# Attention and a feed-forward block on one core: the first feed-forward product of the later passes computed with seven half-deep products for eight, its weight blocks read from DRAM

## The chip, the cores and the metric

The kernel runs on one core of one Trainium2 chip. The metric is the device time of one execution in microseconds (us), as the median of the runs shown. Engines are called as the profile calls them: PE is the matrix engine (PEld its weight loads), DVE the vector engine, ACT the scalar engine, POOL the general-purpose engine, SP the engine that issues nearly all of this kernel's DMAs.

## The reference, cut to what matters

```python
mask   = q_bucket[:, :, :, None] == k_bucket[:, :, None, :]
scores = np.where(mask, scale * np.matmul(q, k.transpose(0, 1, 3, 2)), -1000000000.0)
...
x = attn_out.transpose(0, 2, 1, 3).reshape(B * S, H * D)     # 3072 x 512
h = x @ w_in                                                 # 512 x 2048
g = np.where(pos, h, np.where(neg, 0.0, (h + beta) ** 2 / (4.0 * beta)))
return (g @ w_out).astype(np.float32)                        # 2048 x 512
```

There are 4 batches of 768 tokens and 8 heads of 64. The change touches only how `h = x @ w_in` is computed for batches 1, 2 and 3.

## The kernel before, in words

All matrix products are float32 by splitting: each operand is held as a high part and a low part in the fast 32-bit matmul format (F32R), and a product is the sum of three matmuls, high by high, high by low and low by high.

First comes the attention of all 32 heads, `NU` = 12 work units to a head; it is not changed. Beside it the weights are converted from 64-bit to 32-bit floats: `WeightSplit.steps` makes for each of 16 blocks of `w_in` and of `w_out` a list of steps (DMA of the raw words, four DVE steps and one ACT step, the cast to the high part on ACT, the subtraction that gives the low part), and `conv` hangs each step on a work unit of the attention by a table of offsets. Some blocks are put to DRAM (`stage`, tensors `wd`) and fetched later. The blocks of `w_in` end in `wih` and `wil` (12 tiles of their own, four in tiles that attention gives up), those of `w_out` in `woh` and `wol`.

Then `ffn` runs over units (c, f): c is one of 8 chunks of `CH` = 384 tokens (two chunks to a batch), f one of 16 blocks of 128 hidden columns. `gemm1` issues 12 matmuls of 384 columns (four quarters of the contraction by three) into one of two PSUM banks `h`. ACT makes `t` and `z` from the bank (two ACTIVATEs), DVE finishes the function (one SCALAR_TENSOR_TENSOR, one TENSOR_TENSOR), ACT casts `ghi`, DVE subtracts to `glo`. `gemm2` issues 9 matmuls of 512 columns into three of six PSUM banks `y`; it is called `GLAG` = 3 units behind `gemm1`, so a unit's function has three units of time. `ffn_order` runs the two chunks of batch 0 interleaved (32 units, in which the last `w_out` blocks are still converted), then chunks 2 to 7 one after the other (96 units).

The normalised input of a chunk is made during the chunk before it: `load_x` issues DMAs of the raw rows and of two broadcast factors (`xe`, `xr`), `XMaker.make` has four parts per quarter (DVE, POOL, ACT cast, POOL subtraction). The order on every engine is the order in which the program writes it; each engine takes its instructions strictly in that order, and `prep` and `post` are lists of small pieces that are written just before or just after a unit's `gemm1`.

Of the kernel before, what the change touches and what calls it, by code (L numbers as in the profile page):

```python
# [13 lines left out]
I32 = mybir.dt.int32  # L14
# [27 lines left out]
class WeightSplit:  # L42
# [10 lines left out]
    def steps(self, src, shape, hi, lo, cp, stage=None, low=None):  # L53
# [39 lines left out]

        if stage is None:
            return [s0, s1, s2, s3, s4, s5, s6]

        def put():
            nc.sync.dma_start(out=stage, in_=st["sq"])
# [396 lines left out]
NCT = DM // P  # L495
NF = H * S // P
# [71 lines left out]
def ffn(ctx, tc, wih, wil, woh, wol, xm, xa, xb, out, prep, post):  # L568
# [3 lines left out]
    ps_h = ctx.enter_context(tc.tile_pool(name="ps_h", bufs=2, space=PSUM, reuse_waits="tile"))  # L572
    ps_y = ctx.enter_context(tc.tile_pool(name="ps_y", bufs=6, space=PSUM, reuse_waits="tile"))
    mh = xp.tile([P, 1], F32, name="mh")
# [3 lines left out]
    xc = (xp.tile([P, NCT, CH], F32R, name="xhi"), xp.tile([P, NCT, CH], F32R, name="xlo"))  # L578
    xs = [xa, xb] + [xc, xa] * ((NCH - 2) // 2)

    def piece(name):
        return xp.tile([P, CH], F32, name=name, bufs=2)

    def load_x(c, ct):
        if ct == 0:
            xm.load_sv(c, xp.tile([P, NCT, 2], F32, name="xsv"))
        if c == 1:
            xm.load_raw(c, ct, piece(("xraw", "xraw", "xe", "xr")[ct]))
        else:
            xm.load_raw(c, ct, piece("xraw"))  # L590
            xm.load_er(c, ct, piece("xe"), piece("xr"))

    def gemm1(c, f):
        hi, lo = xs[c]
        ps = ps_h.tile([P, 512], F32, name="h")
        n = 0
        for ct in range(NCT):
            cs = slice(ct * P, (ct + 1) * P)
            for w, x in ((wih[f], hi), (wih[f], lo), (wil[f], hi)):
                nc.tensor.matmul(out=ps[:, 0:CH], lhsT=w[:, cs], rhs=x[:, ct, :], start=(n == 0),  # L600
                                 stop=(n == 3 * NCT - 1))
                n += 1
        t = gp.tile([P, CH], F32, name="t")
        z = gp.tile([P, CH], F32, name="z", bufs=3)
        nc.scalar.activation(out=t, in_=ps[:, 0:CH], func=AF.Relu, scale=0.5, bias=mh)  # L605
        nc.scalar.activation(out=z, in_=t, func=AF.Relu, scale=1.0, bias=m1)  # L606
        nc.vector.scalar_tensor_tensor(out=t, in0=t, scalar=1.0, in1=t, op0=ALU.min, op1=ALU.mult)  # L607
        nc.vector.tensor_tensor(out=z, in0=t, in1=z, op=ALU.add)
        g = [None, None, z]
        to_hi.append(g)  # L610
        return g

    to_hi, to_lo = [], []

    def g_hi(left):

        while len(to_hi) > left:
            g = to_hi.pop(0)
            g[0] = gp.tile([P, CH], F32R, name="ghi", bufs=GLAG)
            nc.scalar.copy(out=g[0], in_=g[2])  # L620
            to_lo.append(g)

    def g_lo():
        while to_lo:
            g = to_lo.pop(0)
            g[1] = gp.tile([P, CH], F32R, name="glo", bufs=GLAG)
            nc.vector.tensor_tensor(out=g[1], in0=g[2], in1=g[0].bitcast(F32), op=ALU.subtract)  # L627

    ys = {}

    def gemm2(c, f, g):
        ghi, glo, _ = g
        if f == 0:
            ys[c] = [ps_y.tile([P, 512], F32, name="y") for _ in range(CH // P)]
        for m in range(CH // P):
            ms = slice(m * P, (m + 1) * P)
            for k, (g_, w) in enumerate(((ghi, woh[f]), (ghi, wol[f]), (glo, woh[f]))):
                nc.tensor.matmul(out=ys[c][m], lhsT=g_[:, ms], rhs=w, start=(f == 0 and k == 0),  # L638
                                 stop=(f == NFT - 1 and k == 2))
            if f == NFT - 1:  # L640
                r0 = c * CH + m * P
                if c == NCH - 1 and m == CH // P - 1:
                    for n, cp in ((0, nc.vector.tensor_copy), (1, nc.scalar.copy)):
                        cs = slice(n * DM // 2, (n + 1) * DM // 2)
                        ot = piece(("xraw", "xe")[n])[:, 0:DM // 2]
                        cp(out=ot, in_=ys[c][m][:, cs])
                        nc.sync.dma_start(out=out[r0:r0 + P, cs], in_=ot)
                    continue
                ot = xp.tile([P, DM], F32, name="ot", bufs=2)
                nc.scalar.copy(out=ot, in_=ys[c][m])  # L650
                nc.sync.dma_start(out=out[r0:r0 + P, :], in_=ot)
# [7 lines left out]
    for ct in reversed(range(NCT)):  # L659
        prep[0].insert(0, (load_x, (1, ct)))  # L660
# [204 lines left out]
```

## Time and profile before

| | us |
|---|---|
| median of 3 runs (lowest to highest) | 1019.07 (1018.93 to 1019.59) |
| profiled execution, its own time | 1019.4 |
| its span | 1017.3 |
| attention ends, first unit of the feed-forward block starts | 473.9 |
| first unit of chunk 2 starts | 603.5 |
| PE busy | 993.6 of 1017.3 |
| DVE, ACT, POOL busy | 695.4, 647.4, 396.5 |

In the rows of the trace the first number is a start in us from the span's start, then a duration. Durations of matmuls overlap, since they are pipelined; the pace of a run of matmuls is read from the chain of work, which gives a start, the length of a piece and its count. The granted clock of PE was 1.00 in every stretch looked at.

### The profile page before, as it was taken

To read this page: it belongs to the slowest core of one execution; us is meant where nothing else is said; L and a number is where in the kernel's file an instruction comes from. 1 tells how busy PE (TensorE), PEld (TensorE's weight loads), DVE (VectorE), ACT (ScalarE), POOL (GpSimd) and SP (SyncE) were. 2 spreads that over 40 slices of the span, in tenths; PEclk is the share of its full clock that TensorE was granted. 3 is DMA by queue.
4 is the path that set the end of the run, shared out by engine and by line. 5 is a ranking of instruction groups with operands and counts; after the bars stand their busy time and mean duration, and the time that the engine had idled before them with its cause. 6 is when DMAs were issued, how large, how long until landed. Compare 5 with 4: busy or idle time off the path is not lost.

```text
span 1017.3 us, 15246 instructions
## 1 busy us (share of the span) xinstructions
PE 993.6 (98%) x5180; PEld 918.3 (90%) x5180; DVE 695.4 (68%) x1106; ACT 647.4 (64%) x1430; POOL 396.5 (39%) x460
## 2 busy tenths in 40 slices
PE   5899999999999999999999999999999999999998
PEld 4789999999999999989999999999999999999997
DVE  7678999999999998895877644544535445355332
ACT  5779988998899998887555544444444444444433
POOL 6666777777887777565000210201202102011000
PEclk9999999999999999999999999999999999999999
DMA  3645666766666666535113102102021021020000
GB/s 93 166 108 155 165 167 175 182 172 168 156 168 164 152 162 171 134 102 166 63 62 109 62 19 79 47 21 81 24 78 47 1 79 47 22 80 24 32 1 32
DMA packets 52806, 100.11 MB, mean 98 GB/s; under 512 B 12920, under 2 KB 34040, under 8 KB 52728
## 3 DMA queue, kind: packets, MB, share of 16 engines
q1 hardware_dynamic: 52512, 99.14, 35.9%
q8 instruction: 41, 0.67, 0.3%
q14 instruction: 37, 0.30, 0.1%
q10 hardware_dynamic: 216, 0.00, 0.0%
HBM read 57.90 MB, written 16.04 MB: 73 GB/s over the span
## 4 chain that ended last, share of the span: by engine, by line
PE 89%; DVE 4%; ACT 3%; DMA 2%; issue 1%; POOL 0%; SPq 0%; DVEq 0%; ACTq 0%
PE y L638 26%; PE h L600 26%; PE smax L258 7%; PE s L298 6%; PE o L332 6%; PE o L330 6%; PE o L331 5%; PE s L297 5%; DVE nm L262 2%; PE o L178 2%; DMA t<-te 1%; DVE nm L359 1%; DMA wraw<-in_w_in_dram 1%; DVE pl L39 0%; ACT ph L306 0%
## 5 line engine op out<-in xcount | busy, mean ns | idle before, releaser
L605 ACT ACTIVATE t<-h,mh 128x384 f32<-128x384 f32 x128 | 74.5, 582 | 272.8 <-PE h L600 272.2
L607 DVE SCALAR_TENSOR_TENSOR t<-t 128x384 f32<-128x384 f32 x128 | 72.6, 567 | 253.5 <-ACT z L606 253.5
L306 ACT ACTIVATE ph<-s 128x384 fp32r<-128x384 f32 x380 | 188.2, 495 | 47.0 <-PE s L298 40.5
L262 DVE TENSOR_REDUCE nm<-smax 128x1 f32<-128x768 f32 x186 | 176.4, 948 | 18.4 <-PE smax L258 16.3
L39 POOL TENSOR_TENSOR pl<-pf,ph 128x384 fp32r<-128x384 f32 x128 | 142.0, 1115 | 77.4 <-ACT pf L311 75.3
L39 DVE TENSOR_TENSOR pl<-s,ph 128x384 fp32r<-128x384 f32 x256 | 135.7, 545 | 13.7 <-ACT s L311 10.0
L297 PE MATMUL s<-t 128*128 128x384 f32 x384 | 132.1, 344 | 0.8 <-DVE t L212 0.8
L550 POOL TENSOR_TENSOR xraw<-xraw,xr 128x384 f32<-128x384 f32 x24 | 24.7, 1027 | 274.8 <-DVE xraw L547 274.8
L298 PE MATMUL s<-t 128*128 128x384 f32 x384 | 130.2, 339 | 0.8 <-DMA t<-te 0.8
L332 PE MATMUL o<-pl,va 128*128 128x386 f32 x384 | 130.4, 340 | 0.2 <-DVE pl L39 0.2
L330 PE MATMUL o<-ph,va 128*128 128x386 f32 x384 | 130.1, 339 | 0.0
L331 PE MATMUL o<-ph,vb 128*128 128x386 f32 x384 | 129.5, 337 | 0.0
L311 ACT ACTIVATE s<-s 128x384 f32<-128x384 f32 x252 | 125.0, 496 | 0.0
L600 PE MATMUL h<-t,wih 128*128 128x384 f32 x480 | 122.9, 337 | 1.0 <-ACT t L605 1.0
L638 PE MATMUL y<-t,ghi 128*128 128x512 f32 x384 | 120.2, 394 | 0.0
L258 PE MATMUL smax<-t 128*128 128x384 f32 x372 | 101.4, 353 | 5.4 <-DVE nm L262 4.5
L600 PEld LDWEIGHTS h<-t,wih 128*128 128x128 f32 x480 | 88.0, 188 | 6.2 <-ACT t L605 1.4
L627 DVE TENSOR_TENSOR glo<-z,ghi 128x384 fp32r<-128x384 f32 x128 | 89.5, 699 | 0.2 <-ACT ghi L620 0.2
L258 PEld LDWEIGHTS smax<-t 128*128 128x128 f32 x372 | 64.0, 188 | 21.9 <-DVE nm L262 20.8
L638 PEld LDWEIGHTS y<-t,ghi 128*128 128x128 f32 x384 | 71.4, 188 | 11.4
L606 ACT ACTIVATE z<-t,m 128x384 f32<-128x384 f32 x128 | 79.0, 617 | 4.1
L600 PE MATMUL h<-t,wil 128*128 128x384 f32 x240 | 80.9, 337 | 0.0
(130 smaller groups left out, 2106.6 us busy)
## 6 DMA issues: line engine op xcount, KB each, us to landing
t<-t SPq DMA_DIRECT2D x60, 384.0 KB
raw<-in_qk_dram SPq DMA_DIRECT2D x15, 768.0 KB
wraw<-in_w_in_dram SPq DMA_DIRECT2D x16, 512.0 KB
wraw<-in_w_out_dram SPq DMA_DIRECT2D x16, 512.0 KB
xd<-xs SPq DMA_DIRECT2D x32, 192.5 KB
vraw<-in_v_dram SPq DMA_DIRECT2D x16, 384.0 KB
out_dram<-ot SPq DMA_DIRECT2D x23, 256.0 KB
xraw<-xd SPq DMA_DIRECT2D x26, 192.0 KB
```

The lines of the kernel that those rows point to most:

```text
L39: eng.tensor_tensor(out=out, in0=a, in1=b, op=ALU.subtract)
L258: nc.tensor.matmul(out=smax[hd][:, hf, 0:HS], lhsT=t2[:, 0, h, i * P:(i + 1) * P], rhs=t2[:, 1, h, hf * HS:(hf + 1) * HS], start=True, sto ...
L262: nc.vector.tensor_reduce(out=nmp(hd)[:, i:i + 1], in_=smax[hd][:, :, 0:HS], axis=AX.XY, op=ALU.max, negate=True)
L297: nc.tensor.matmul(out=ps[:, 0:HS], lhsT=t1[:, 1, h, ks], rhs=t1[:, 0, h, sl], start=True, stop=False)
L298: nc.tensor.matmul(out=ps[:, 0:HS], lhsT=t2[:, 1, h, ks], rhs=t2[:, 0, h, sl], start=False, stop=True)
L306: nc.scalar.activation(out=ph[:, 0:HS], in_=ps[:, 0:HS], func=AF.Exp, scale=SCALE)
L311: nc.scalar.activation(out=pf, in_=ps[:, 0:HS], func=AF.Exp, scale=SCALE)
L330: nc.tensor.matmul(out=o, lhsT=wa, rhs=ph, start=(jj == 0), stop=False)
L331: nc.tensor.matmul(out=o, lhsT=wb, rhs=ph, start=False, stop=False)
L332: nc.tensor.matmul(out=o, lhsT=wa, rhs=pl, start=False, stop=(jj == NJ - 1))
L600: nc.tensor.matmul(out=ps[:, 0:CH], lhsT=w[:, cs], rhs=x[:, ct, :], start=(n == 0), stop=(n == 3 * NCT - 1))
L638: nc.tensor.matmul(out=ys[c][m], lhsT=g_[:, ms], rhs=w, start=(f == 0 and k == 0), stop=(f == NFT - 1 and k == 2))
```

## The change

For batches 1 to 3 the first product is taken over pairs: two blocks of hidden columns (2i and 2i+1), two halves of the contraction and the two chunks of a batch make a 2 by 2 by 2 scheme of eight half-deep products; the kernel now forms seven (`PRODUCTS`), each of 6 matmuls of 384 columns. This needs sums of inputs (four per half of the contraction, `x_sum`), sums of weights (four blocks out of four, `w_sum`) and sums of results: three products accumulate in PSUM on top of an earlier one, ACT copies one bank out and DVE adds five times per seven products.

Weights: the converted 32-bit blocks are also written to DRAM (`wq`, for the 12 blocks that were not staged before, at offset 16 of the table). In the first 32 units the kernel writes the three plain half blocks of each pair to DRAM tensors `wc` (`w_plan`, `w_plain`), fetches pairs back into a scratch tile `tmp` (`w_get`), forms the four sums (`w_sum`), splits them (`w_hi` on ACT, `w_lo` on DVE) and writes them to `wc` (`w_put`): pairs 0 to 2 in the first 32 units (the put of pair 2 stands at product 0), pairs 3 to 7 during products 0 to 28. Each product then reads its weight block (128 by 512 floats, high and low) from `wc` into a ring of 9 slots, 9 products ahead (`w_load`).

Inputs: 14 operands (7 combinations, high and low) per half of the contraction are made one batch ahead, on DVE and ACT alone (`x_plan`: raw rows, factors `x_er`, `x_norm`, `x_sum`, `x_hi`, `x_lo`); POOL has no work left in this part.

Second product: its matmuls go into one queue (`queue_out`), and `issue` writes 4 to 6 of them behind each product, 36 per seven products. There are 3 x 8 x 7 = 168 products.

PE, one unit of the last chunk before. `h` is the PSUM bank of the first product, `y` those of the second, `x12` is a count:

```order
L638 MATMUL y<-wol_6035,ghi 128x512
L638 MATMUL y<-woh_6034,glo 128x512
L600 MATMUL h<-t_1_78,t_2_76 128x384 x12
L638 MATMUL y<-woh_6036,ghi 128x512
L638 MATMUL y<-wol_6037,ghi 128x512
L638 MATMUL y<-woh_6036,glo 128x512
```

PE in the change, two products in the first of the three later batches; `wbig` holds operands, `t_1_75` is a slot of the ring:

```order
L867 MATMUL h_6066<-wbig,t_1_75 128x384 x6
L657 MATMUL y<-woh_6045,ghi 128x512
L657 MATMUL y<-wol_6046,ghi 128x512
L657 MATMUL y<-woh_6045,glo 128x512
L657 MATMUL y<-woh_6047,ghi 128x512
L657 MATMUL y<-wol_6048,ghi 128x512
L867 MATMUL h_6065<-wbig,t_1_75 128x384 x6
L657 MATMUL y<-woh_6047,glo 128x512
```

A group of 12 has become groups of 6 that alternate between the two banks, with five matmuls of the second product between them.

DVE, two units before (`t`, `z`, `glo` are the function's tiles, `xraw` a piece of input being normalised):

```order
L607 SCALAR_TENSOR_TENSOR t<-t 128x384
L608 TENSOR_TENSOR z<-t,z 128x384
L627 TENSOR_TENSOR glo<-z,ghi 128x384
L547 SCALAR_TENSOR_TENSOR xraw<-xe,xsv,xraw 128x384
L607 SCALAR_TENSOR_TENSOR t<-t 128x384
```

DVE in the change around products 19 and 20 of the 168; L881, L884 and L887 read a PSUM bank (`h`) that PE wants back, `sumw` are weight sums from `tmp`, `pc` pieces of input:

```order
L632 TENSOR_TENSOR glo<-z,ghi 128x384
L623 SCALAR_TENSOR_TENSOR t<-t 128x384
L624 TENSOR_TENSOR z<-t,z 128x384
L39 TENSOR_TENSOR sumw<-tmp 128x512
L884 TENSOR_TENSOR wa<-wa,h_6066 128x384
L623 SCALAR_TENSOR_TENSOR t<-t 128x384
L624 TENSOR_TENSOR z<-t,z 128x384
L39 TENSOR_TENSOR sumw<-tmp,sumw 128x256
L39 TENSOR_TENSOR sumw<-sumw,tmp 128x256
L686 SCALAR_TENSOR_TENSOR pc_6073<-pc_6075,xsva,pc_6073 128x384
L688 TENSOR_TENSOR pc_6073<-pc_6073,pc_6076 128x384
L887 TENSOR_TENSOR wsq<-h_6065,wsq 128x384
```

The readings of the PSUM banks now stand on DVE behind the function of the product before and behind pieces of weight and input work.

SP in the change, DMAs at products 4 to 6 (`wc<-tmp` is `w_put`, `tmp<-wq` is `w_get`, `<-wc` is `w_load`):

```order
L746 DMA wc_100<-tmp 128x4x256
L747 DMA wc_100<-tmp 128x4x256
L830 DMA t_1_75<-wc_98 128x512
L647 DMA out_dram<-ot 128x512
L830 DMA t_1_75<-wc_99 128x512
L647 DMA out_dram<-ot 128x512 x2
L730 DMA tmp<-wq_89 128x2x256
L731 DMA tmp<-wq_90 128x512
```

The fetch of the next pair stands two products behind the put of the pair before, and uses the same tile.

The diff, cut:

```diff
+PRODUCTS = ((0, 0, 0), (5, 4, 1), (1, 1, 0), (4, 5, 1), (3, 3, 0), (6, 2, 1), (2, 6, 0))
+NRING = 9
...
-    return steps + [(c, f) for c in range(2, NCH) for f in range(NFT)]
+    return steps
...
+    def x_norm(b, cc, k):
+        ct, sv = 2 * (k % 2) + cc, spc[b % 2]
+        nc.vector.scalar_tensor_tensor(out=pc[k], in0=pc[4], scalar=sv[:, ct, 0:1], in1=pc[k],
+                                       op0=ALU.mult, op1=ALU.add)
+        nc.vector.tensor_tensor(out=pc[k], in0=pc[k], in1=pc[5], op=ALU.mult)
...
+    def x_plan(b, cc, raw, norm, made):
+        at(raw, x_raw, b, cc)
+        after(raw, x_er, b, cc, 0)
+        for k, n in enumerate(norm):
+            at(n, x_norm, b, cc, k)
+            if k < 3:
+                after(n, x_er, b, cc, k + 1)
+        for o, n in made:
+            if o in SUMS:
+                at(n, x_sum, o)
+            after(n, x_hi, b, cc, o)
+            at(n + 1, x_lo, b, cc, o)
...
+    def w_put(i):
+        nc.sync.dma_start(out=wc[i][:, 3:7, 0], in_=hi_w.bitcast(F32))
+        nc.sync.dma_start(out=wc[i][:, 3:7, 1], in_=raw_w.bitcast(F32))
+
+    def w_plan(i, n):
+        at(n, w_get, i)
+        at(n + 1, w_sum, 0)
+        at(n + 2, w_sum, 1)
+        at(n + 2, w_sum, 2)
+        for t in range(2):
+            after(n + 2 + t, w_hi, t)
+            at(n + 3 + t, w_lo, t)
+        at(n + 4, w_put, i)
...
+    for i in range(NFT // 2):
+        at(8 + i, w_plain, i)
+        w_plan(i, (20, 24, 28)[i] if i < 3 else N1 + 6 * (i - 3))
+    x_plan(1, 0, 9, (11, 13, 15, 17), ((0, 18), (1, 18), (3, 19), (2, 19), (4, 20), (5, 21), (6, 21)))
+    x_plan(1, 1, 22, (24, 25, 26, 27), ((0, 27), (1, 28), (3, 28), (2, 29), (4, 29), (5, 30), (6, 30)))
+    for b in (2, 3):
+        t0 = N1 + 56 * (b - 2)
+        for cc in range(2):
+            t = t0 + (14, 35)[cc] - (8 if b == 3 else 0)
+            x_plan(b, cc, t, [t + 2 + 2 * k for k in range(4)],
+                   [(o, t + 10 + k) for k, o in enumerate((0, 1, 3, 2, 4, 5, 6))])
...
+    def w_load(k):
+        if k < NK:
+            nc.sync.dma_start(out=ring[k % NRING].bitcast(F32),
+                              in_=wc[k // NBLK % (NFT // 2)][:, PRODUCTS[k % NBLK][0]].rearrange("p t n -> p (t n)"))
...
+    def late(k, g):
+        stage[1].append((k + 1, act_out, g))
+        stage[2].append((k + 2, g_hi, g))
+        stage[3].append((k + 3, g_lo, g))
...
+    for k in range(NK):
+        b, i, s = 1 + k // 56, k % 56 // NBLK, k % NBLK
+        blk, o, bank = PRODUCTS[s]
+        ps = hb[(bank + i) % 2][:, 0:CH]
+        for n in (3, 2, 1):
+            due(n, k)
+        for fn, a in prep.pop(N1 + k, ()):
+            fn(*a)
+        w = ring[k % NRING]
...
+                nc.tensor.matmul(out=ps, lhsT=w[:, cs], rhs=x, start=(n == 0 and s not in (2, 3, 6)),
+                                 stop=(n == 5), skip_group_check=True)
...
+        w_load(k + NRING)
+        if s == 0:
+            nc.scalar.copy(out=cm, in_=ps)
+        elif s == 1:
+            nc.vector.tensor_tensor(out=cu, in0=ps, in1=cm, op=ALU.add)
+        elif s == 2:
+            src, c, f = ps, 0, 0
+        elif s == 3:
+            nc.vector.tensor_tensor(out=cv, in0=ps, in1=cm, op=ALU.add)
+        elif s == 4:
+            nc.vector.tensor_tensor(out=cm, in0=ps, in1=cv, op=ALU.add)
+            src, c, f = cm, 1, 1
+        elif s == 5:
+            nc.vector.tensor_tensor(out=cv, in0=cv, in1=ps, op=ALU.subtract)
+            src, c, f = cv, 1, 0
+        else:
+            nc.vector.tensor_tensor(out=cu, in0=ps, in1=cu, op=ALU.add)
+            src, c, f = cu, 0, 1
+        if src is not None:
+            g = act_in(src)
+            late(k, g)
...
+        issue(6 if s == 6 else 4 if 3 <= k < 6 else 5)
...
-        conv((2 * i + 3) * NU, wi_steps(i, nc.scalar), (0, 7, 9, 13, 15, 17, 19))
+        conv((2 * i + 3) * NU, wi_steps(i, nc.scalar), (0, 7, 9, 13, 15, 16, 17, 19))
```

Here `act_in` writes the two ACTIVATEs, `act_out` the two DVE steps, `g_hi` and `g_lo` the cast and the subtraction; N1 is 32, and a number n in `at(n, ...)` or `after(n, ...)` above 31 means product n - 32.

More of the change, by code (lines that the diff above doesn't have):

```diff
@@ L606, in gemm1 @@
[L606 to L651, printed above, removed]
@@ L688, in lsh_attn_ffn @@
+    for k in range(NK, NK + 4):
+        for n in (3, 2, 1):
+            due(n, k)
+        if k < NK + 3:
+            issue(5)
+    issue(len(queue))
+    assert not prep and not post
 @with_exitstack
```

251 lines of the change are left out of this document (192 added, 59 removed).

## The prediction

> **What bounds the kernel now.** I read the page first, then the busy time by stretches, then the chain of waits.
>
> ```profile
> PE 993.6 (98%) x5180; PEld 918.3 (90%) x5180; DVE 695.4 (68%) x1106; ACT 647.4 (64%) x1430; POOL 396.5 (39%) x460
> PE 89%; DVE 4%; ACT 3%; DMA 2%; issue 1%; POOL 0%; SPq 0%; DVEq 0%; ACTq 0%
> ```
>
> ```profile
> core 0: us, PE busy (x) PEld busy (x) DVE busy (x) ACT busy (x) POOL busy (x), PEclk, DMA share, GB/s
> 60.00:440.00 380.00, 378.33 (x2108) 363.57 (x2107) 353.06 (x519) 340.58 (x816) 283.32 (x324) 1.00 0.62 160
> 473.90:603.50 129.60, 128.56 (x648) 116.56 (x647) 89.22 (x154) 67.89 (x129) 11.49 (x10) 1.00 0.24 74
> 603.50:1009.00 405.50, 405.50 (x2025) 366.56 (x2024) 181.43 (x314) 171.28 (x327) 43.65 (x40) 1.00 0.14 42
> ```
>
> PE carries 89% of the chain. The stretch that the change rewrites is the last: 405.5 us in which PE never pauses, at full clock, while DVE and ACT work less than half the time and DMA moves 42 GB/s. Its pace stands in the chain:
>
> ```profile
> 607.74 2.12 PE h L600 x12
> 609.86 2.10 PE y L638 x9
> ```
>
> So a matmul of the first product (384 columns) takes 2.12/12 = 0.176 us of PE and one of the second (512) 2.10/9 = 0.233. A unit is 4.2 us, 96 units 404 us. Time leaves this stretch only by fewer matmuls, and comes back only as PE pauses.
>
> **What is removed.** 96 units had 1152 first-product matmuls; 168 products of 6 have 1008. 144 x 0.176 = 25.3 us. That is the whole gain there can be. The second product keeps its 9 per unit.
>
> **What is added on DVE.** These rows give its costs, free of POOL:
>
> ```profile
> 489.46 0.69 DVE L39 TENSOR_TENSOR t<-wsq,t 128x512 fp32r<-128x512 f32 x1
> 490.06 0.56 DVE L39 TENSOR_TENSOR t<-xraw,t 128x384 fp32r<-128x384 f32 x1
> ```
>
> ```profile
> L39 DVE TENSOR_TENSOR pl<-s,ph 128x384 fp32r<-128x384 f32 x256 | 135.7, 545 | 13.7 <-ACT s L311 10.0 <-PE o L331 2.6 <-POOL pl L39 1.0
> ```
>
> ```profile
> 715.10 0.58 ACT L605 ACTIVATE t<-h,mh 128x384 f32<-128x384 f32 x1 [2.15 <-PE h L600]
> 715.71 0.62 ACT L606 ACTIVATE z<-t,m 128x384 f32<-128x384 f32 x1
> 716.36 0.56 DVE L607 SCALAR_TENSOR_TENSOR t<-t 128x384 f32<-128x384 f32 x1 [1.23 <-ACT z L606]
> 716.96 0.56 DVE L608 TENSOR_TENSOR z<-t,z 128x384 f32<-128x384 f32 x1
> 717.43 0.55 DVE L627 TENSOR_TENSOR glo<-z,ghi 128x384 fp32r<-128x384 f32 x1
> 721.63 1.38 DVE L627 TENSOR_TENSOR glo<-z,ghi 128x384 fp32r<-128x384 f32 x1
> ```
>
> From start to start: a dependent 384-column step 0.60, an independent one 0.47, 512 columns 0.60. A step that reads PSUM lasts 545 ns, as the others do: 0.5. The 1.38 is a step beside POOL work; with POOL gone it falls away, which is worth nothing, since DVE does not set the end there. Per seven products (a pair) DVE has four functions at 0.60 + 0.47 + 0.47 = 1.54 and five PSUM adds at 0.5, 8.7 us. PE's pair is 42 x 0.176 + 36 x 0.233 = 15.8 us. A set of inputs (half a contraction, one batch) adds four normalisations at 1.1 and 11 sums and subtractions at 0.47, 9.7; weight sums add 2.5 per pair (one step of 512 columns, two of 256 counted 0.35 each, two of 512).
>
> DVE keeps its order, and that makes waits. After each of three adds per pair (products s = 4, 5, 6) ACT must do t and z, 0.58 + 0.62 and 0.14 between, before DVE's next step; a `glo` of 0.47 fits into that twice. That is 3 x 1.34 - 2 x 0.47 = 3.1 us of standing still per pair, whenever DVE is behind. A plain pair is then 11.8 of 15.8 us and costs nothing: PE's own matmuls hide it.
>
> What may be late: a product's bank is wanted again two products on, 5 x 0.233 + 6 x 0.176 + 5 x 0.233 = 3.4 us after its last matmul. The add takes 0.55, so DVE may run 2.8 us late; some 2.5 where it enters a bit late. Behind that, PE waits.
>
> **The crowded stretch, products 19 to 29,** holds pair 6's and pair 7's weight sums and inputs for batch 2 together. DVE there: 7 `glo`, 7 function pairs and 8 adds 14.8, two weight groups 5.0, two normalisations 2.2, five subtractions and three sums 3.8: 25.8 us. ACT waits: six, four covered by a `glo`, 6 x 1.34 - 4 x 0.47 = 6.2. Sum 32.0. PE: 66 x 0.176 + 57 x 0.233 = 24.9. The excess of 7.1 less 2.5 is 4.6: I take 5. Bounds: 0, if steps slip into the ACT waits better than the written order lets them, and 7.
>
> **The three other input sets** (from products 35, 62 and 83): seven products hold 8.7 + 11 x 0.47 + 3.1 = 17.0 against 15.8. The excess of 1.2 is less than the allowance, but the four normalisations before have used most of it. I take 1 each, 3; bounds 0 and 8 (2.5 each if nothing is left over).
>
> **The change-over.** The DMA costs come from three output blocks of 256 KB in a quiet place:
>
> ```profile
> L650 ACT COPY ot<-y x3: 578/587/587, 750.3 to 753.0; 128x512 f32<-128x512 f32 x3
> 750.88 3.04 SPq L651 DMA_DIRECT2D out_dram<-ot  x3
> GB/s 0 0 0 0 0 0 49 385 401 393 401 418 49 0 0 0 0 98 418 393 140 3 8 54 129 246 277 246 123 135 184 154 117 129 240 166 191 148 277 295
> ```
>
> The slices are 0.25 us from 750. Data flow at 400 GB/s, 0.65 us per 256 KB. There are two `ot` buffers, so I read the third copy, at 753.0, as freed by the first DMA, issued at 750.88: 2.1 us, of which 1.45 is not transfer. At product 0 DVE ends pair 2's last subtraction 3.7 us after the last plain unit (1.3 for ACT, 1.1, a `glo` behind a late cast 0.7, 0.6). Its put (512 KB) needs 1.45 + 1.3 and lands at 6.5; the fetch of pair 3 needs the same tile, two DMAs, 0.35 + 2.1 and some, 9.1; `w_sum` 0.6 and the add 0.55 stand behind it on DVE: 10.2. PE wants that bank (product 1's) at 2.10 + 1.06 + 1.17 + 1.06 + 3.4 = 8.8. Pause 1.5. In the later rounds fetch and sum have three products, 6.8 us, and the allowance: 0.
>
> The Trainium skill (DMA: Bandwidth & Descriptors, section "Anatomy of one DMA — SWDGE (gpsimd) path") gives 2.0 us fixed plus bytes at 436 GB/s per DMA, most of it the write receipt, worst when DRAM is the target; it was fitted on another issuing engine. By it, as an estimate, 256 KB take 2.6 us where the row has 2.1, put and fetch each gain 0.5, and the sum would be 1 us higher. I keep the row.
>
> **Queueing of DMAs.** Products 14 to 22 want per product 0.26 MB of ring, 1.57 MB per six of weight traffic and 2.36 MB per nine of inputs, together 0.79 MB in 2.25 us, 350 GB/s against the 400 seen. Factors and fetches land late there. I take 1.5; bounds 0 and the last rival below. The ring, nine products or 20 us ahead, hides its own loads.
>
> **At nothing.** The 32 plain units: DVE 89 us gets two input sets and three weight groups, 27, and is at 116 of 130; a unit's function may take three units, 12.6 us, and needs 4. Attention: 12 puts of 256 KB beside 160 GB/s at a DMA share of 0.62, hidden by that; without cover 12 x 0.65 = 8. POOL's 44 us leave a path that they were not on. The end (last matmul to end of span) stays.
>
> **Sum.** 1019.4 - 25.3 + 5 + 3 + 1.5 + 1.5 = 1005.1 against the profiled execution's own time (span 1017.3, 2.1 around it), which is 0.3 above the median: **1005**. The bounds that these terms carry: 994 with no pause, 1018 with 7 + 8 + 1.5 and 8 in the attention.
>
> **Rivals.**
>
> *All pauses hidden.* 1019 - 25 + 1: 995. For it: DVE is at 181 of 405 us, and a plain pair has 4 us to spare. Against: the crowded stretch is over 100% by count, whatever the average.
>
> *The puts in the attention cost.* They stand on SP among the small transfers on which PE waits there:
>
> ```profile
> PE s L298 <- DMA t<-te: 0.8, 2, 0.6
> ```
>
> If each put delays one of those by its 0.65 us: 1005 + 8 = 1013. Against: such waits are 0.8 us in all now, with larger DMAs around.
>
> *Slow round trips through DRAM: slower than before.* One mechanism: DMA under this load runs at the 160 GB/s of the attention and not at 400. Put and fetch of 1.57 MB then take 9.9 us and two times 1.45, 12.8 in all. The room in a later round is 6.8 + 2.5, so PE loses 3.5 in each of four, 14, and 8 at the change-over (room 4.8). Factors and one ring block, 0.65 MB, take 4.1 us and not the 2.2 in which these rows issue them:
>
> ```profile
> 714.64 0.45 SPq L532 DMA_DIRECT2D xe<-ed  x1
> 716.41 0.60 SPq L533 DMA_DIRECT2D xr<-rd  x1
> ```
>
> That is 1.9 late for 12 normalisations (the first of each set is covered), 23. Together 45: 1019 - 25 + 45 = 1039. It breaks even where the losses are 25, at about 215 GB/s. For it: in 380 us of attention the rate stays at 160. Against: the share there is 0.62, so 160 is what was asked for, about 258 at full share.
>
> That fewer matmuls are not issued can be left out: the order on PE has the 168 groups of six.
>
> **How the numbers follow.** Chances: the forecast (pauses of 6 to 16 us, 1000 to 1010) 0.53; all hidden 0.15; attention 0.12; nothing gained or lost, by a milder form of the last rival, 0.05; slow round trips 0.15. The first three are faster: 0.80; same 0.05; slower 0.15. About 0.2% is what a measurement of this kernel can tell from no change. The range 995 to 1018 holds the first three, and leaves out the slow cases and the lower tip.
>
> **What would show it.** Right: in the products' stretch PE pauses only before a product's first matmul, released by DVE, most of them between products 19 and 30, some 11 us in all; matmul pace 0.176 and 0.233; granted clock 1.00; the stretch 379 + 11 us where 404 were; attention and the 32 units within 1 us. Wrong: pauses released by DMA; normalisations or weight sums on DVE that wait for DMA by over 2 us each; pauses in plain pairs (then the chain DVE, ACT, DVE is longer than counted); a pause at the ring.

## The result, and the profile after

| | before | changed |
|---|---|---|
| time, median (lowest to highest), us | 1019.13 (1018.93 to 1019.59), 4 runs | 1050.26 (1047.72 to 1052.2), 4 runs |
| ratio, 95% interval | | 1.030 [1.027, 1.033] |
| profiled execution, its own time / span, us | 1019.4 / 1017.3 | 1052.17 / 1050.4 |
| attention ends | 473.9 | 480.9 |
| the 32 plain units, to the start of the stretch behind them | 129.6 | 136.4 |
| stretch of units or products, to the last first-product matmul | 401.5 | 416.5 |
| from there to the end of the span | 12.3 | 16.6 |

The change makes the kernel 3.0% slower; 1005 us was forecast. The executions of the changed kernel also scatter more, 4.5 us against 0.7. Most experiments below are single executions, so differences of less than 5 us between them are read from their waits and not from their times.

The page of the changed kernel, busy times (part 1) and the chain of work that ended last (part 4):

```profile
PE 984.1 (94%) x5036; PEld 893.3 (85%) x5036; DVE 793.7 (76%) x1356; ACT 681.1 (65%) x1489; POOL 344.3 (33%) x412
PE 60%; DVE 14%; DMA 12%; ACT 8%; issue 3%; SPq 2%; POOL 0%; DVEq 0%; ACTq 0%
```

PE has 144 matmuls fewer and 9.5 us less busy time, but its share of the chain falls from 89% to 60%; DMA rises from 2% to 12%. The busy times by stretches (columns as before: stretch, length, busy of PE, PEld, DVE, ACT, POOL, granted clock, DMA share, GB/s), for a stretch of the attention, the plain units and the products:

```profile
60.00:440.00 380.00, 373.03 (x2069) 356.48 (x2068) 344.77 (x510) 334.35 (x801) 278.55 (x318) 1.00 0.65 166
480.90:617.30 136.40, 129.83 (x647) 116.35 (x646) 103.79 (x194) 72.87 (x140) 2.54 (x2) 0.99 0.55 177
617.30:1033.80 416.50, 388.26 (x1864) 338.75 (x1863) 263.57 (x516) 195.33 (x367) 0.00 (x0) 0.99 0.53 155
```

PE is idle for 7.0 and 6.6 us in the first two, where it was 1.7 and 1.0 before, and in the products, where it never was, it is idle for 28 of 416.5 us while DVE works 264. What PE waited for there, and what DVE waited for there (total, times, longest):

```profile
PE h L867 <- DVE wsq L875: 14.6, 9, 5.5
PE h L867 <- DVE wsq L887: 5.1, 4, 2.4
PE h L867 <- DVE wsq L881: 3.3, 2, 1.8
PE h L867 <- DVE wa L884: 3.0, 3, 1.9
```

```profile
DVE t L623 <- ACT z L618: 94.1, 82, 2.2
DVE wsq L881 <- PE h L867: 22.2, 19, 2.0
DVE pc L686 <- DMA pc<-ed: 14.6, 7, 5.8
DVE sumw L39 <- DMA tmp<-wq: 12.3, 4, 6.5
DVE pc L688 <- DMA pc<-rd: 4.0, 6, 1.0
```

PE's longest waits name a DVE step that reads a product's bank (L867 is the product); those on ACT are at most 0.6 us each. DVE, in turn, stands 31 us for transfers: factors (`ed`, `rd`) and fetched pairs of weights (`wq`). The wait for ACT's `z` is larger, but it is as large (97.4 us) in the kernel without these transfers (below), where the products lose only 10.2 us.

To set the losses against places, take the start of each product minus the start of the one before, less the pace without pauses (2.22 us, 2.45 behind the seventh of a pair). The excess is 39.6 us: 8.6 at products 0 to 5, 14.5 at 19 to 31, 4.6 at 41 to 52, 6.9 at 66 and 67, the rest at 10 and between 79 and 101. One pause read in full, at the change-over: SP's issues, DVE and PE.

```profile
622.14 0.37 SPq L747 DMA_DIRECT2D wc<-tmp  x1
625.09 0.56 SPq L730 DMA_DIRECT2D tmp<-wq  x1
625.70 0.59 SPq L731 DMA_DIRECT2D tmp<-wq  x1
```

```profile
622.03 0.55 DVE L632 TENSOR_TENSOR glo<-z,ghi 128x384 fp32r<-128x384 f32 x1
629.13 0.69 DVE L39 TENSOR_TENSOR sumw<-tmp 128x512 f32<-128x512 f32 x1 [6.55 <-DMA tmp<-wq]
629.74 0.55 DVE L875 TENSOR_TENSOR wsq<-h,wsq 128x384 f32<-128x384 f32 x1
```

```profile
630.35 1.97 PE L867 MATMUL h<-wbig,wraw 128*128 128x384 f32 x5 [5.50 <-DVE wsq L875]
```

The second half of the put of pair 2 (512 KB) is issued at 622.14, the fetch into the same tile 2.95 us later, and DVE's sum starts 4.04 us after that. SP issues nothing between put and fetch. The add that frees the bank stands behind the sum, and PE behind the add. The rate of the DMA engines in slices of 0.25 us from 622.0 to 632.0:

```profile
GB/s 340 279 4 0 233 352 352 344 348 344 123 0 0 0 0 0 0 4 98 41 279 377 418 414 377 262 229 270 172 254 337 348 385 418 213 209 172 148 16 0
```

The put's data is through at 624.75; then nothing moves for 1.5 us, and the bulk of the fetch runs from 627.0 at up to 418 GB/s. So the rate is high while data flow. Of the put's 2.95 us some 1.75 are data, 0.9 pass before the first byte and 0.3 behind the last; the fetch's bulk starts 1.9 us behind its first issue, and two blocks of the ring, issued at 626.38 and 626.86, share the engines with it.

A second kind of pause, near 800 us: SP's issues for an input set of batch 3, then the DVE step that waits for the last of them, then PE.

```profile
788.60 0.56 SPq L672 DMA_DIRECT2D xsvb<-xd  x1
789.25 3.40 SPq L675 DMA_DIRECT2D pc<-xd  x4
792.74 0.38 SPq L830 DMA_DIRECT2D t<-wc  x1
793.16 1.10 SPq L682 DMA_DIRECT2D pc<-ed  x2
794.31 1.24 SPq L682 DMA_DIRECT2D pc<-rd  x2
```

```profile
797.57 0.62 DVE L686 SCALAR_TENSOR_TENSOR pc<-pc,xsvb,pc 128x384 f32<-128x384 f32 x1 [5.83 <-DMA pc<-ed]
```

```profile
799.78 1.27 PE L867 MATMUL h<-t,wraw 128*128 128x384 f32 x3 [5.07 <-DVE wsq L875]
```

SP alone needs 7.0 us to issue these ten transfers. One of the four pieces of raw rows takes 1.79 us of this, the others 0.38 to 0.60; why is not shown. The normalisation stands two products, 4.5 us, behind their first issue in the program. SP came to them late as well: they are written for product 62, but two output blocks, issued at 787.63 and 788.21, stood ahead. In the other three sets SP needs 4.7 to 5.5 us for nearly the same transfers, and DVE's longest waits are 2.7, 2.0 and 1.4 us.

Behind each of these pauses PE ran at half its clock (stretches chosen at the clock's steps; the clock is the third column from the end):

```profile
615.60:619.00 3.40, 3.40 (x11) 3.03 (x10) 3.37 (x8) 2.20 (x6) 0.00 (x0) 0.50 0.52 200
629.20:636.00 6.80, 5.65 (x16) 5.28 (x17) 5.02 (x10) 1.75 (x3) 0.00 (x0) 0.50 0.60 191
```

A third such stretch of 3.4 us begins at 799.9. Together 13.6 us at half speed, 6.8 us lost, some 5 of them in the products. The first follows this pause of the last plain unit:

```profile
614.77 0.50 PE L657 MATMUL y<-woh,glo 128*128 128x512 f32 x1 [3.06 <-DVE glo L632]
```

### The profile page after: what moved, and what is told of

The parts are those of the page before. It is cut to its first block, busy times and chain, and to the rows that moved or that the text cites. A ratio compares the mean times of both kernels' runs of the same rounds, so it can differ in the third digit from the quotient of the medians.

```text
span 1050.4 us, 15678 instructions
## 1 busy us (share of the span) xinstructions
PE 984.1 (94%) x5036; PEld 893.3 (85%) x5036; DVE 793.7 (76%) x1356; ACT 681.1 (65%) x1489; POOL 344.3 (33%) x412
## 4 chain that ended last, share of the span: by engine, by line
PE 60%; DVE 14%; DMA 12%; ACT 8%; issue 3%; SPq 2%; POOL 0%; DVEq 0%; ACTq 0%
PE y L657 14%; PE h L867 11%; PE smax L258 5%; PE s L298 5%; PE o L332 5%; PE o L330 5%; PE o L331 5%; PE s L297 5%; DMA t<-te 5%; PE h L772 3%; DMA pc<-rd 3%; DVE t L623 2%; ACT t L617 2%; ACT z L618 2%; DVE nm L262 2%
## 5 line engine op out<-in xcount | busy, mean ns | idle before, releaser
L331 PE MATMUL o<-ph,vb 128*128 128x386 f32 x384 | 129.6, 337 | 0.0
L657 PE MATMUL y<-t,ghi 128*128 128x512 f32 x384 | 125.1, 397 | 0.6 <-ACT ghi L628 0.6
L628 ACT CAST ghi<-z 128x384 fp32r<-128x384 f32 x129 | 65.1, 505 | 47.2 <-DVE z L624 42.0
L867 PE MATMUL h<-wbig,t 128*128 128x384 f32 x399 | 83.6, 342 | 6.3 <-DVE wsq L887 4.0
L617 ACT ACTIVATE t<-wsq,mh 128x384 f32<-128x384 f32 x48 | 29.6, 617 | 90.3 <-DVE wsq L881 56.3
L867 PEld LDWEIGHTS h<-wbig,t 128*128 128x128 f32 x399 | 71.6, 190 | 15.5 <-DVE wsq L887 5.2
L298 PEld LDWEIGHTS s<-t 128*128 128x128 f32 x384 | 72.4, 189 | 10.9 <-DMA t<-te 10.7
L867 PE MATMUL h<-wbig,wraw 128*128 128x384 f32 x321 | 68.2, 347 | 13.9 <-DVE wsq L875 6.7
```

The costliest lines, as they stand in the source:

```text
L298: nc.tensor.matmul(out=ps[:, 0:HS], lhsT=t2[:, 1, h, ks], rhs=t2[:, 0, h, sl], start=False, stop=True)
L331: nc.tensor.matmul(out=o, lhsT=wb, rhs=ph, start=False, stop=False)
L657: nc.tensor.matmul(out=ys[c][m], lhsT=g_[:, m * P:(m + 1) * P], rhs=w, start=(first and k == 0), stop=(last and k == 2))
L867: nc.tensor.matmul(out=ps, lhsT=w[:, cs], rhs=x, start=(n == 0 and s not in (2, 3, 6)), stop=(n == 5), skip_group_check=True)
```

## The experiments

Theory A: DVE stands behind transfers that come late, holds PSUM banks meanwhile, and PE pauses. Theory B: DVE's own steps and its waits for ACT set the pace, as the prediction had it. Theory C: the DMA rate is too low. In the attention: the puts by their place on SP, or by their bytes.

### Leaving out one half of the feeding at a time

```diff
-        w_plan(i, (20, 24, 28)[i] if i < 3 else N1 + 6 * (i - 3))
+        if i < 3:
+            w_plan(i, (20, 24, 28)[i])
```

> Left out: the weight rounds of pairs 3 to 7 (fetch, sums, split, put); their products read the blocks of pairs 0 to 2. Theory A (DVE stands waiting for transfers that SP issues late and that need some 4 us, and holds PSUM banks meanwhile): the 8.6 us of pauses at products 0 to 5 go, and about half of the 14.6 us at products 19 to 31; those at 41 to 52, 66 to 67 and 79 to 101 (16 us together) stay. About 1034 us. Theory B (DVE's own steps and its waits for ACT set the pace where the stretch is crowded): only the crowded stretch gets shorter, by up to 11, and the pauses at 0 to 5 go; 1031 too, but no pause behind a transfer is left. Theory C (rate of the DRAM traffic): the input sets' transfers no longer share it, and the pauses at 66 to 67 shrink as well; about 1025.

Measured: 1030.16 us. The loss at products 0 to 5 falls to 0.9 and that at 19 to 31 to 4.8; those at 41 to 52 and 79 to 101 stay (4.7 and 4.0), and that at 66 to 67 goes from 6.9 to 5.5. A smaller loss there is what C asked for, but 1.4 us is little of it.

```diff
-    for b in (2, 3):
+    for b in ():
```

> Left out: the input sets of batches 2 and 3; their products read batch 1's operands. Theory A: the pauses at 41 to 52 (4.6), 66 to 67 (6.9) and 79 to 101 (4.5) go, and half of the 14.6 at 19 to 31; the 8.6 at 0 to 5 stay. About 1050 - 23 = 1027 us. Theory B: the same places, but the four sets cost only the 8 us that the count of DVE steps gives; about 1042. Theory C: weight rounds without the sets' traffic are no longer late either; the pauses at 0 to 5 shrink too, about 1020.

Measured: 1029.84 us. The loss at 0 to 5 stays (7.4), 7.6 us follow up to product 30, nothing behind it. As A had it, not as C. Each half costs some 20 us. The second run lies near A's 1027 and not at B's 1042, but both leave out DVE steps together with the transfers; the next one does not.

### Leaving out the transfers and keeping every DVE and ACT step

```diff
-        at(n, w_get, i)
+        if i < 3:
+            at(n, w_get, i)
...
-        at(raw, x_raw, b, cc)
-        after(raw, x_er, b, cc, 0)
+        if b == 1:
+            at(raw, x_raw, b, cc)
+            after(raw, x_er, b, cc, 0)
```

(`w_put` and the later `x_er` in the same way.)

> Left out, in the products' stretch: only the transfers of the weight rounds (fetches and puts) and of the input sets (raw rows and factors). Every DVE and ACT step stays where it is and works on what lies in its tile; products read the blocks of pairs 0 to 2. Theory A: nearly all 39.6 us of loss in the products go, down to the 5 to 8 that DVE's own work was counted at, and the half clock at 629 and 800 us with them: 1016 to 1020 us. Theory B: DVE's work is unchanged, so most of the loss stays: over 1040 us. Theory C makes the same forecast as A here; it is told apart by the rate that the transfers show.

Measured: 1018.5 us. The products' stretch of this kernel:

```profile
612.60:999.70 387.10, 379.80 (x1863) 335.11 (x1863) 263.84 (x518) 195.38 (x367) 0.00 (x0) 1.00 0.43 123
```

DVE is busy for 263.84 us where the changed kernel has 263.57: the same work, in a stretch 29.4 us shorter, with no half clock. The excess over the pace is 10.2 us: 6.6 at products 19 to 31, 1.06 at each of 51 to 52, 79 to 80 and 100 to 101, the rest small. So 29.4 of the 39.6 us come from transfers: 8.1 at products 0 to 5, 7.9 at 19 to 31, 3.5 at 41 to 52, 6.9 at 66 and 67 and 2.3 at 79 to 101. 10.2 come from DVE's own work.

### The puts in the attention

The kernel before with `put` added as a step at offset 16, nothing else:

```diff
-            return [s0, s1, s2, s3, s4, s5, s6]
+            return [s0, s1, s2, s3, s4] + ([put] if keep is not None else []) + [s5, s6]
...
-        conv((2 * i + 3) * NU, wi_steps(i, nc.scalar), (0, 7, 9, 13, 15, 17, 19))
+        conv((2 * i + 3) * NU, wi_steps(i, nc.scalar), (0, 7, 9, 13, 15, 16, 17, 19))
```

> The kernel before with one thing added: the 12 puts of 256 KB during the attention. If the later end of the attention (480.9 us where it was 473.9) comes from the puts, which stand on SP ahead of the small transfers that PE waits for: attention ends 6 to 7 us later, about 1026 us. If it comes from something else in the change (tiles laid out in another way): within 1 us of 1019.

Measured: 1025.84 us beside 1020.29 of the kernel before on the same chip; attention ends at 479.8. SP's issues around one put, and PE's wait for the small transfer in 60 to 440 us (0.8 before):

```profile
97.30 1.15 SPq L157 DMA_DIRECT2D t<-t  x2
98.55 1.17 SPq L95 DMA_DIRECT2D wq<-wsq  x1
99.82 1.96 SPq L282 DMA_DIRECT2D t<-te  x1
```

```profile
PE s L298 <- DMA t<-te: 4.0, 11, 0.8
```

The put's issue takes 1.17 us of SP, directly ahead of `t<-te`, and that of `t<-te`, 3 KB, takes 1.96 where it takes 1.2 in the kernel before. The weight loads of the same matmul wait 8.9 us (1.5 before). Place and bytes are told apart by moving the put, in the changed kernel, to offset 26 and then to 20:

```diff
-            return [s0, s1, s2, s3, s4] + ([put] if keep is not None else []) + [s5, s6]
+            return [s0, s1, s2, s3, s4, s5, s6] + ([put] if keep is not None else [])
...
-        conv((2 * i + 3) * NU, wi_steps(i, nc.scalar), (0, 7, 9, 13, 15, 16, 17, 19))
+        conv((2 * i + 3) * NU, wi_steps(i, nc.scalar), (0, 7, 9, 13, 15, 17, 19, 26))
```

> The whole computation; only the 12 puts of the attention stand ten units later in SP's order, where SP is otherwise idle for 2.7 us. If they cost by their place (1.2 us of SP ahead of the small transfer that PE waits for): attention ends 5 to 6 us earlier, about 1045 us. If they cost by their bytes: no change.

Measured: 1059.81 us, a miss: attention ends at 488.7. PE no longer waits for `t<-te`, but ACT has a new wait in the attention:

```profile
ACT wsq L69 <- DMA wq<-wsq: 21.6, 9, 3.3
```

The put holds the scratch tile `wsq` (two buffers) until the next block's conversion wants it. At offset 20 it stands behind the load of raw rows and is soon over:

> The whole computation; only the 12 puts of the attention stand four units later, behind the load of raw rows, and not ten (which made ACT wait for the scratch buffer that the put still read, 21.6 us in nine waits). If place on SP is what they cost: waits of PE for the small transfer go back from 6.2 us to under 2, ACT does not wait for a put, attention ends at 475 to 476 us, about 1045 us in all. If they cost wherever they stand: attention still ends after 479.

Measured: 1043.0 us, attention ends at 472.9, where the kernel before has 473.9, with the same twelve puts. So the cost is one of place and not of bytes; the issue of a put at offset 20 still takes up to 1.4 us, but no small transfer that PE waits for stands behind it.

### Giving transfers more time

```diff
-            x_plan(b, cc, t, [t + 2 + 2 * k
+            x_plan(b, cc, t - 3, [t + 2 + 2 * k
```

> The whole computation; only the raw rows and first factors of the four input sets of batches 2 and 3 are issued three products earlier. Theory A (SP needs 7 us to issue these ten transfers, the last lands some 2 us later, and the first normalisation stands two products, 4.5 us, behind): DVE's wait of 5.8 us at 797 us goes, with it the loss of 6.9 at products 66 to 67, the half clock there, and some 2 at the other three sets: 1040 to 1043 us. If the transfers were slow by rate and not by their place on SP: they are slow earlier too, and the time changes by less than 3.

Measured: 1053.84 us, a miss. DVE's wait at products 66 to 67 is gone, but products 64 to 65 lose 6.0: the raw rows now stand on SP among the output blocks of the batch before, and ACT stands behind an output transfer, since there are two `ot` buffers for six blocks:

```profile
792.76 0.59 ACT L646 COPY ot<-y 128x512 f32<-128x512 f32 x1 [4.34 <-DMA out_dram<-ot]
```

At products 15 to 17 the set's raw rows stand ahead of a fetch on SP, and DVE waits 5.15 us for that. The wait was passed on twice.

The weight rounds alone (`w_get` and `w_sum` get times of their own):

```diff
-        w_plan(i, (20, 24, 28)[i] if i < 3 else N1 + 6 * (i - 3))
+        w_plan(i, (16, 23, 29)[i] if i < 3 else N1 + 7 * i - 18, (20, 26, 31)[i] if i < 3 else N1 + 7 * i - 15)
```

> The whole computation; only the times of the eight weight rounds are changed: sums two to four units or three products behind the fetch (one before), a round every seven products instead of six. Theory A: the wait of DVE for the fetched pair goes, so the 8.6 us at products 0 to 5, the pause of 3.06 in the last plain unit with its half clock (5), and a third of the 14.6 at products 19 to 31: about 1032 us. Theory B (DVE's own work sets it): as much work in as many us, so only the pause at the change-over goes: over 1042.

Measured: 1040.67 us, 10 of the 18 forecast. In the products no wait of `sumw` for a fetch is left, nor a loss at 0 to 5, and 19 to 31 lose 10.2 instead of 14.5. The sets still lose: 6.7 at 66 to 68, and 2.2 at 41, where the changed kernel had 0.3. The plain units take 136.0 us, hardly less than 136.4: the 5 us forecast there did not come, since DVE now waits 5.33 us for a factor at 589 us.

These rounds, the put at offset 26, and the sets' normalisations three products apart, together:

> All three together, and normalisations three products apart instead of two. Theory A: the gains add, 6 in the attention, 5 in the plain units, about 30 in the products, which keep the 10 that DVE's own work and its waits for ACT cost; 1008 to 1012 us, faster than the kernel before. Theory B or C: over 1025.

Measured: 1041.81 us, ratio to before 1.022 [1.020, 1.024]: a miss by 30. The attention ends at 487.4 (the put at 26), and the products still lose 21.3, among them 3.7 at product 64, where ACT stands at an output block as in the kernel with earlier raw rows, and 5.9 at 14 to 17, where DVE waits 4.01 us for a factor.

Six places for output blocks instead of two (spare columns of `pcs`, and `wraw` for the first chunk):

```diff
-        ot = xp.tile([P, DM], F32, name="ot", bufs=2)
+        ...
+            ot = early[m]
+        else:
+            ot = ots[m if c % 2 else 3 + m]
```

> The whole computation; only the output blocks get six places in SBUF instead of two. Theory: ACT stands up to 6 us behind the output transfer of the block two before, because SP issues that late, and the function of the next product stands behind ACT. Then the pause near 600 us (1.76) and 1.5 at the end go, and a part of the loss at products 8 to 10: 1046 to 1048 us. Rival: these waits are covered; within 1 us of 1050.

Measured: 1046.14 us. ACT has no wait for an output transfer left; the pause near 600 us, which stood behind this one of the changed kernel, is gone:

```profile
599.41 0.58 ACT L646 COPY ot<-y 128x512 f32<-128x512 f32 x1 [5.53 <-DMA out_dram<-ot]
```

The gain of 4 us is of the size of the scatter and is read from the stretches, not from the time: the plain units take 133.4 us (136.4 in the changed kernel), the end 13.9 (16.6). The products lose as much as before.

### Another issuing engine

```diff
-                nc.sync.dma_start(out=t[64 * h:64 * h + 64], ...
+                nc.gpsimd.dma_start(out=t[64 * h:64 * h + 64], ...
```

(`w_get` and `w_put` in the same way.)

> The whole computation; only the issuing engine of three kinds of transfer (factors, fetches, puts of the weight sums) is changed from SP to POOL, which has no work there; times in the program stay. If the delay is SP's (half a us of issue for each transfer, in order behind waits of the ring's loads for PE): DVE's waits for transfers shrink to less than half of 43 us and the products lose about 20 us instead of 39.6: about 1030 us. If it is the transfers' own latency and their sharing of the DMA engines: 1045 to 1060.

Measured: 1057.66 us. The change-over as POOL issues it, and DVE's wait for it:

```profile
625.54 0.76 POOL L747 DMA_DIRECT2D wc<-tmp  x1 [1.38 <-DVE tmp L39]
630.26 0.71 POOL L730 DMA_DIRECT2D tmp<-wq  x1 [3.96 <-DMA wc<-tmp]
630.97 0.57 POOL L731 DMA_DIRECT2D tmp<-wq  x1
```

```profile
634.00 0.69 DVE L39 TENSOR_TENSOR sumw<-tmp 128x512 f32<-128x512 f32 x1 [8.28 <-DMA tmp<-wq]
```

From put to fetch 4.7 us, from fetch to sum 3.7: the round trip is no shorter on a queue without other work, and DVE's waits for transfers do not shrink (32.7 us in the products, 30.9 before). This run alone does not clear SP's order, since a put issued by POOL may take longer of its own (4.7 us against 2.95). But at the change-over SP too had issued nothing between put and fetch, so there the transfers' own time sets the weight round. The set at products 66 to 68 loses 3.1 instead of 6.9, with raw rows and factors issued by two engines at once: there SP's serial issue did count, as far as one run shows. ACT as issuing engine was not tried.

### All remedies together

Puts at offset 20; six places for output; the low part of the sums written into `sumw` instead of into the fetched pair, so that the next pair can be fetched as soon as the sums are formed; three to six products from fetch to sum; sets kept away from outputs and fetches:

```diff
-        sub(nc, nc.vector, raw_w[:, sl], sum_w[:, sl], hi_w[:, sl].bitcast(F32))
+        sub(nc, nc.vector, sum_w[:, sl], sum_w[:, sl].bitcast(F32), hi_w[:, sl].bitcast(F32))
...
+        w_plan(i, (14, 22, 27)[i] if i < 3 else N1 + (0, 8, 15, 22, 29)[i - 3], (20, 25, 30)[i] if i < 3 else N1 + 7 * i - 15)
...
+            t = t0 + ((9, 36) if b == 2 else (12, 34))[cc]
```

> The whole computation, all remedies together: puts four units later, six places for output, sums kept apart from the fetched pair so that a pair is fetched three to six products ahead of its sums, a round every seven products, normalisations three or four products apart and away from the fetches and outputs. Theory A: no wait of DVE for a transfer over 2 us in the products, no half clock, some 10 us left that DVE's own work costs; attention to 475, plain units 131: 1008 to 1013 us, faster than the kernel before by 0.6 to 1.1%. If DVE's waits only move elsewhere again: over 1025.

Measured: 1014.29 us, ratio 0.995 [0.993, 0.996]. Excess in the products 18.7 us; 5.7 of it at products 14 to 16, where DVE waits 4.42 us for a factor that was issued behind a put.

Then the same with the sets spread further (batch 2's first raw rows at product 7, ahead of that put; the fetch of pair 4 at product 10 instead of 8; batch 3's work over 44 products):

> The version with all remedies, and its input sets spread further: batch 2's first raw rows and factors two products earlier, ahead of a put and a fetch instead of behind them; batch 3's normalisations and sums over 44 products instead of 41, with gaps. If the late factors made the loss at products 14 to 16: 5 us of it go, and 2 to 3 more at products 85 to 107: 1006 to 1010 us. If the transfers only collide elsewhere: no gain over 1014.

Measured: 1006.81 us, ratio 0.987 [0.985, 0.988]: faster than the kernel before by 1.3%. Its plain units and its products' stretch (the cuts lie 0.5 us early), and all that PE waited for in the latter:

```profile
474.10:603.30 129.20, 128.17 (x647) 116.23 (x646) 106.29 (x200) 74.35 (x143) 2.56 (x2) 1.00 0.57 184
603.30:990.90 387.60, 380.34 (x1863) 334.91 (x1862) 260.33 (x510) 192.89 (x364) 0.00 (x0) 1.00 0.55 167
```

```profile
PE h L877 <- DVE wsq L897: 4.0, 6, 1.2
PE h L877 <- DVE wsq L885: 2.5, 2, 1.2
PE h L877 <- DVE wa L894: 0.2, 1, 0.2
```

All the transfers are there, at 167 GB/s where the changed kernel moved 155, and the clock is 1.00. So the mean rate was not what limited the changed kernel.

> The same, and left out in the products: fetches, puts, raw rows and factors (products read the blocks of pairs 0 to 2); all DVE and ACT steps stay. If DVE's work is what is left: within 3 us of the version with its transfers, and pauses at the same products. If transfers are: products lose under 5 us, about 1000.

Measured: 1002.71 us; excess 6.7 us where the version with its transfers has 10.6, at the same products (17, 24, 29, 36, 57). So 3.9 us are still transfers, just over the 3 that the first branch allowed, and the larger part is DVE's own work, most of it in pairs that also carry a weight round or a set.

## Why the prediction was wrong

In the products the sum held 3 us for late transfers (1.5 for the change-over, 1.5 for queueing, nothing for the later rounds and for the first normalisation of a set). They cost 29.4. Outside the products it held nothing, and 18 us came: 7.0 in the attention, 6.8 in the plain units, 4.3 at the end. These are the terms that failed; the gain and DVE's own work held.

**The gain: right.** The matmuls are gone, and where PE does not pause, the stretch shortens as counted. 379 + 11 us was the forecast for the products; without late transfers they take 387.1 and 387.6 to the start of the last matmul, about 1 us short of the whole.

**DVE's own work: right in kind, place and size.** 5 for the crowded stretch, where 6.6 stay with the transfers left out, and 1 for each of the other three sets, where 1.06 stay. With what is left elsewhere that is 10.2 for a forecast of 8, within the bounds of 0 to 15.

**Later weight rounds, at 0.** "In the later rounds fetch and sum have three products, 6.8 us, and the allowance": three products lie between the put and the sum, but only one between the fetch and the sum, and the trip was taken as shorter than it is (0.35 + 2.1 us and some from fetch to sum, where the four rounds show 3.9 to 4.1 whenever DVE waited). In three of the four rounds DVE came to the sum late itself and waited 0.5 us at most. For the last one it waited 4.78 us:

```profile
686.36 0.37 SPq L747 DMA_DIRECT2D wc<-tmp  x1
690.85 0.56 SPq L730 DMA_DIRECT2D tmp<-wq  x1
694.70 0.69 DVE L39 TENSOR_TENSOR sumw<-tmp 128x512 f32<-128x512 f32 x1 [4.78 <-DMA tmp<-wq]
```

Those are 8.3 us from put to sum, where the table has 6.8. With a wait of 2.69 us for a factor at product 19, this one stands in the crowded stretch, where the transfers cost 7.9 us in all.

**The change-over, at 1.5.** Its mechanism was right in every step, put, fetch, sum, add, and its size wrong: a pause of 5.50 us, 8.6 with what follows it at half clock. Part of the miss lay ahead of the put. Pair 2's own fetch had stood behind the put of pair 1 until 606.55, and DVE waited for it among the plain units:

```profile
611.09 0.69 DVE L39 TENSOR_TENSOR sumw<-tmp 128x512 f32<-128x512 f32 x1 [5.24 <-DMA tmp<-wq]
```

So the put of pair 2 left SP 10.9 us behind the last matmul of the last plain unit's first product, where 3.7 were forecast; 3.9 of these PE lost as well, by its pause and the half clock behind it. The put then took 2.95 (2.75 forecast). The row behind the estimate was a write of 256 KB. For the fetch, issue to sum took 4.04 where 2.5 and some were held. The profile before has twelve fetches of 256 KB (`wsq<-wd`), of which one can be read alone: issued at 490.23, its data run from 491.0 to 492.5, so they are in 2.3 us behind the issue, with nothing else moving. For two fetches with ring blocks among them the bound should have been wide. The Trainium skill (DMA: Bandwidth & Descriptors, section "Anatomy of one DMA — SWDGE (gpsimd) path") gives 2.6 us for 256 KB by its fixed cost and rate, as an estimate; the second of the two fetches took 3.43 from its issue at 625.70, so the page's figure would have been too small here too, though nearer.

**"The first of each set is covered".** In the set near 800 us it was the worst wait of all its normalisations, 5.83 us: SP's 7.0 us of issue, begun late behind two output blocks, against 4.5 us of room. Two of the other three sets show first waits of 2.0 and 1.2 us. SP's 0.45 and 0.60 us per issue stand in the prediction's own rows; they were added up for four factors (2.2 us), and not for the ten transfers ahead of a set's first normalisation.

**Queueing at 1.5, bounds up to the last rival.** What it was to cover is part of the 29.4 us; fetches and sets delay each other, as the kernel with earlier raw rows shows.

**Attention at nothing.** It cost 7.0 us. The rival that priced it at 8 was right in place and in what is delayed: puts on SP among the small transfers that PE waits for. Its size was near by luck: it counted 0.65 us of data per put, but the same bytes cost nothing at offset 20, and what delays is SP's issue, 1.17 us for the put and 0.7 more for the small transfer behind it. The cover that I named, the DMA share of 0.62, was of the wrong resource; SP's order had none.

**The 32 plain units at nothing, and the end "stays".** 6.8 and 4.3 us. In the units two waits stood in no term: ACT behind an output transfer, and the fetch of pair 2 behind the put of pair 1. At the end the two chunks of a batch close together and six blocks go out, not three; with six places for them 2.7 of the 4.3 us go.

**The clock at 1.00.** The 6.8 us at half clock were in no term. The Trainium skill (TensorE: Matmul & The Clock Gate, section "Part 1: The HAM clock gate (the “warmup” mystery)") says that PE falls to half rate after about one idle window of 3.4 us, in windows that run freely. The trace agrees in the lengths, 3.41 and 6.83 us of half clock, one and two windows, but not in the whole idle window: the pause of 3.06 us is shorter than one. Laid out in windows of 3.41 us by the clock's own steps, the traces of all these runs show 36 stretches of half clock between the end of the attention and the last 5 us. Each begins behind a window in which PE was idle for 1.7 to 3.4 us (2.6 for the one at 615.56 above); of some 2800 windows at full clock that were not followed by one, none was idle for more than 1.9 us. So about half a window is enough, and here the measurement decides. A pause of 3.20 us in the kernel without transfers fell on two windows, 1.4 and 1.8 us, and had no half clock behind it.

**The rivals.** The slow one named the right place, round trips through DRAM ahead of a DVE that holds banks, and its sign; by the rate of 160 GB/s it was wrong, since the fetch ran at up to 418. So its 1039 us, the nearest of the numbers on record, is in part luck. What "would show it wrong" was seen: DVE waiting for DMA by over 2 us. "All hidden" falls by the 10.2 us that stay without transfers. That the well-spaced version ends near the number forecast does not make the forecast right: it is another kernel, with each of the costs above removed one by one.

## What to carry to other kernels

Count a transfer's time from the place of its issue in the queue to the step that uses it: the issues ahead of it on SP at 0.3 to 0.6 us each here, single ones at 1.2 to 2.0, then some 3 to 4 us for a fetch of 256 to 512 KB, and compare that with the steps that the program's table puts between the two. A step that waits for a transfer on an in-order engine holds everything behind it, PSUM banks too, so one late transfer costs PE its whole lateness less a small allowance, and a pause can cost again by the clock: one of 2.08 us, in the kernel with three remedies, was followed by 3.4 us at half clock. Moving one transfer passes the wait on to the next in the queue; only giving all of them room, and freeing the buffers that tie a fetch to the put before it, turned 3.0% slower into 1.3% faster.

## What was not expected of the hardware

The time that SP needs to issue one transfer does not go by its bytes: 0.32 us for most ring blocks of 256 KB, 0.37 for a put of 512 KB, 0.45 to 0.6 for most factors broadcast to 64 rows. Nor is it fixed for one kind: a put of 256 KB took 1.17 us in the attention behind two large transfers and 0.33 to 0.35 at other places, a transfer of 3 KB took 0.7 to 2.0, one piece of raw rows 1.79 beside 0.38. What makes an issue long is not shown. Between the last byte of a put and the first bulk bytes of a fetch into the same tile lay 2.25 us (624.75 to 627.0), in which almost nothing moved.
